# A Fourier layer and two expert layers on one core: tile sizes, conversion pace and the first blocks' order are changed

## The chip, the cores and the metric

The kernel runs on one core of one Trainium2 chip. The metric is the device time of one execution in microseconds. The profile is of one execution; its times are counted from the first instruction. PE is TensorE's matmul row and PEld its weight loads, DVE is VectorE, ACT is ScalarE, POOL is GpSimd, SP is SyncE, which issues all DMAs here.

## The reference

Two batches of 3008 tokens with 256 features go through a Fourier layer, and the 6016 tokens then through two expert layers with 2048 hidden features. The weights of the expert layers come as float64.

```python
X = np.fft.rfft(x, axis=1)                       # x: (2, 3008, 256)
Yr = Xr @ w_r - Xi @ w_i + b_r
Yi = Xr @ w_i + Xi @ w_r + b_i
Yr, Yi = sign(Y) * max(abs(Y) - 0.01, 0)         # each of the two
y = np.fft.irfft(Yr + 1j * Yi, n=3008, axis=1)
h = y.reshape(6016, 256) @ w_in                  # first expert layer
y1 = (h * np.cos(h)) @ w_out
h = y1 @ w_in2                                   # second expert layer
out = (h * np.clip(h + 3, 0, 6) / 6) @ w_out2
```

## The kernel before

Every product is made of float32r halves: a tensor `a` is kept as `hi` (rounded) and `lo` (the rest), and a product is hi·hi + hi·lo + lo·hi, three matmuls of 128 rows, 128 columns of weights and up to 512 moving columns.

**Transform.** 3008 = 47·64. For each batch, stage A (`a_part`, L334) multiplies eight chunks of x with a table: 16 short matmuls a chunk with 96 moving columns; the result goes to `zh`, `zl`. Then twelve steps `k2_step` work on two frequencies each. A step has twelve matmuls `w_mm` (L398, moving operand `wh` or `wl`), six `b_mm` (L421, moving `ph`), three `v_mm` (L452, moving `sh` or `sl`). Between them ACT and DVE split, add the bias and shrink; `shrink_lo` (L446) forms `sl` on POOL. `v_store` sends a block to DRAM (`u_dram`). What is left of the last steps (`drain`, a list of twelve pieces) is done one piece after each `a_part` of the next batch, or between the first units of the expert layers. `load_u` fetches a group of the transform's output and its table (`u_sb`, `tg_sb`), `y_part` (L286) makes 376 tokens of it, half of the features at a time, into the token tiles `y_sb`. Block 0 of 512 tokens needs groups 0 and 1, block 1 group 2 as well.

**Conversion.** Each expert weight is turned from float64 bits into hi and lo by `convert`. A chunk is 128x512 values; either layer has 16. A step of `Converter` issues one of five DVE instructions (clamp L154, shift L157, top L160, exponent L163, rest L166); with them go ACT's magnitude (L151) and hi (L170) and POOL's sum (L167) and lo (L173). After `rest` the next chunk is loaded into a `raw` tile, 512 KB. `RATE_A`, `RATE_W` say how many steps go with each `a_part` and each k2 step below `PW`; `RATE_1`, `RATE_2` how many go with each unit of the expert layers, `RATE_1` for the units of the first layer on blocks 0 to 2. `cv.require` does at once what a matmul needs and is not yet converted. Before: 34 steps in each batch's twelve k2 steps and 9 in stage A, 77 in all, or 15 chunks.

**Expert layers.** A unit is one block of tokens (eleven of 512, one of 384) and one of 16 groups of 128 hidden features: six matmuls `mm_h` (L577, moving operand the token tiles), the activation on ACT and DVE, a split into `gh` (ACT L620) and `gl` (DVE L621), and, four units later, six matmuls `mm_out` (L634, moving operand `gh`, `gl`, `gh` twice). `groups` orders the units: blocks 0, 1, 2 of the first layer alone, then a block of the first and one of the second layer in turns, unit by unit, and the second layer's last three alone.

PE, ACT and SP take their instructions in the order in which the code issues them; DVE's and POOL's are put in order by the framework's planner.

**Place in SBUF.** The tiles of the pool `persist` stand one behind another; a size is rounded up to 32 bytes per partition. Up to `first` every tile starts at 128 bytes past a multiple of 512. `first` has 8 bytes, which take 32. So `raw`, `cva`, `cvb`, `gh`, `gl`, `o`, `u_sb` and `tg_sb`, which follow it, start at remainder 160; `sh` and `sl` share the slots of `gh` and `gl`. `tg_sb` has 1504 bytes, and 1504 + 32 is a multiple of 512: what follows it (`zh`, `ph`, `wh`, the later token tiles, the second layer's weights) is at 128 again, as are the first layer's weights and the first token tiles.

Of the kernel before, what the change touches and what calls it, by code (L numbers as in the profile page):

```python
# [9 lines left out]
F32 = mybir.dt.float32  # L10
F32R = mybir.dt.float32r
BF16 = mybir.dt.bfloat16
I32 = mybir.dt.int32
U32 = mybir.dt.uint32
AF = mybir.ActivationFunctionType
ALU = mybir.AluOpType
# [9 lines left out]
TP = 2 * N1  # L26
ROWS = 2 * DOF
LAM = 0.01
TWO_PI = 2.0 * math.pi
YPAIRS = 4  # L30
BLOCK_TOKENS = [512] * 11 + [384]
A_CHUNKS = [4] * 8
NFC = DFF // 128
LEAD = 3
DELAY = 4
WARM = 9


RATE_A = (0, 1)
RATE_W = (1, 2, 2)  # L40
RATE_1 = ((1, 0),) * 7 + ((0, 0),)
RATE_2 = ((1, 0), (1, 1))
LATE, CC, CV0 = [1, 3, 4], 5, 7
XB = 3
PW = 12
YP = (0, 3, 6)
YE = 3


# [64 lines left out]
def fourier_moe_moe_kernel(ctx, tc, x, w_r, w_i, b_r, b_i, ta, tg, fg, win1, wout1, win2, wout2, out):  # L114
    nc = tc.nc
    pe, act, dve, sp = nc.tensor, nc.scalar, nc.vector, nc.sync

    def f32(ap):
        return ap.bitcast(F32)

    persist = ctx.enter_context(tc.tile_pool(name="persist", bufs=1))
# [13 lines left out]

    def convert(src, dst_hi, dst_lo, name):

        raw = persist.tile([128, 512, 2], I32, tag="raw", bufs=3, name=f"raw{name}")
        a = persist.tile([128, 512], F32, tag="cva", bufs=2, name=f"cva{name}")
        b = persist.tile([128, 512], F32, tag="cvb", bufs=1, name=f"cvb{name}")  # L140
        au, bu = a.bitcast(U32), b.bitcast(U32)
        w_lo, w_hi = raw.bitcast(U32)[:, :, 0], raw.bitcast(U32)[:, :, 1]

        def load():
            if len(src.shape) == 2:
                sp.dma_start(raw.rearrange("p f two -> p (f two)"), src)
            else:
                sp.dma_start(raw.rearrange("p (a f) two -> p a (f two)", a=2), src)

        def magnitude():  # L150
            act.activation(a, raw.bitcast(F32)[:, :, 1], AF.Abs)  # L151

        def clamp():
            dve.tensor_scalar(a, a, T_MIN, T_MAX, op0=ALU.max, op1=ALU.min)  # L154

        def shift():
            dve.tensor_scalar(au, au, 3, 0x3FFFFFF8, op0=ALU.logical_shift_left, op1=ALU.bitwise_and)  # L157

        def top():
            dve.scalar_tensor_tensor(au, w_hi, 0xC0000000, au, op0=ALU.bitwise_and, op1=ALU.bitwise_or)  # L160

        def exponent():
            dve.tensor_scalar(bu, au, 0xFF800000, None, op0=ALU.bitwise_and)  # L163

        def rest():
            dve.scalar_tensor_tensor(b, w_lo, float(2.0**-52), b, op0=ALU.mult, op1=ALU.mult)  # L166
            nc.gpsimd.tensor_tensor(a, a, b, op=ALU.add)  # L167

        def hi():
            act.activation(dst_hi, a, AF.Copy)  # L170

        def lo():
            nc.gpsimd.tensor_tensor(dst_lo, a, f32(dst_hi), op=ALU.subtract)  # L173

        return dict(load=load, magnitude=magnitude, clamp=clamp, shift=shift, top=top, exponent=exponent, rest=rest, hi=hi, lo=lo)
# [78 lines left out]
    YT = YPAIRS * TP  # L254
# [5 lines left out]
    def groups_of(j):  # L260

        return range(-(-starts[j] // YT), -(-starts[j + 1] // YT))

    u_sb, tg_sb, y_sb, x1_sb = {}, {}, {}, {}


    def token_set(pool, i):
        return [[pool.tile([128, MAXT], F32R, name=f"tok{i}_{e}{z}") for z in range(2)] for e in range(2)]

    free_sets = [token_set(persist, i) for i in range(2)]  # L270

    def load_u(g):
        if g >= NG:
            return
        b, p0 = divmod(g * YPAIRS, NPAIR)
        ut = persist.tile([ROWS, YPAIRS, D], F32, tag="u_sb", name=f"u_sb{g}")
        sp.dma_start(ut, u_dram[b][:, :, p0 : p0 + YPAIRS, :].rearrange("s f i e -> (s f) i e"))
        tt = persist.tile([ROWS, YT], F32, tag="tg_sb", name=f"tg_sb{g}")
        sp.dma_start(tt, tg[:, p0 * TP : (p0 + YPAIRS) * TP])
        u_sb[g], tg_sb[g] = ut, tt  # L280

    def y_part(g, ec):

        yp = psum.tile([128, 512], F32, tag="h", bufs=4, name=f"yp{g}_{ec}")
        for i in range(YPAIRS):
            pe.matmul(  # L286
                yp[:, i * TP : (i + 1) * TP],
                lhsT=u_sb[g][:, i, ec * 128 : (ec + 1) * 128],
                rhs=tg_sb[g][:, i * TP : (i + 1) * TP],
                start=True,  # L290
                stop=True,
            )
        for j in range(NBLK):
            t0, t1 = max(g * YT, starts[j]), min((g + 1) * YT, starts[j + 1])
            if t0 < t1:
                if j not in y_sb:
                    y_sb[j] = free_sets.pop(0)
                yh, yl = (z[:, t0 - starts[j] : t1 - starts[j]] for z in y_sb[j][ec])
                src = yp[:, t0 - g * YT : t1 - g * YT]
                act.activation(yh, src, AF.Copy)  # L300
                dve.tensor_tensor(yl, src, f32(yh), op=ALU.subtract)
        if ec == 1:
            load_u(g + 1)


    with ExitStack() as actx:
        apool = actx.enter_context(tc.tile_pool(name="apool", bufs=1))
        with tc.manual_schedule(engines={mybir.EngineType.PE, mybir.EngineType.SP, mybir.EngineType.Activation}):
# [4 lines left out]
            for b in range(NB):  # L313
                p0 = 0
# [35 lines left out]
            warm = persist.tile([128, 2, D], BF16, tag="r", bufs=3, name="warm")  # L350
            dve.memset(warm, 0.0)

            first = persist.tile([128, 2], F32, name="first")
            act.activation(first, warm[:, 0, 0:2], AF.Sin)
            wp = psum.tile([128, 2, D], F32, tag="acc0", bufs=2, name="wp")
            for i in range(WARM):
                pe.matmul(wp, lhsT=warm[:, 0, 0:128], rhs=warm, start=True, stop=True)
# [28 lines left out]
            ph_t, pp_t, bp_t, u_t, sh_t, vp_t = {}, {}, {}, {}, {}, {}  # L386
# [42 lines left out]
            def shrink_a(b, p):  # L429

                u_t[b, p] = persist.tile([128, 2, D], F32, tag="r", bufs=3, name=f"u{b}_{p}")
                act.activation(u_t[b, p], bp_t[b, p], AF.Relu, bias=-LAM, scale=1.0)  # L432
# [10 lines left out]

            def shrink_lo(b, p):
                sh, sl = sh_t[b, p]
                nc.gpsimd.tensor_tensor(sl, u_t.pop((b, p)), f32(sh), op=ALU.subtract)  # L446

            def v_mm(b, p):
                vp = psum.tile([128, 2, D], F32, tag="acc1", bufs=2, name=f"vp{b}_{p}")
# [16 lines left out]
            def k2_step(b, p):  # L466
                if p < NP:
                    w_mm(b, 2 * p)
                if p >= 2:
                    bias_add(b, p - 2)  # L470
                    shrink_a(b, p - 2)
                    cv.step(RATE_W[0] if p < PW else 0)
                    shrink_b(b, p - 2)
# [9 lines left out]
                if p < NP:  # L483
                    w_mm(b, 2 * p + 1)
                    cv.step(RATE_W[1 + p % 2] if p < PW else 0)
                    w_split(b, 2 * p + 1)
# [21 lines left out]
            for b in range(NB):  # L508
# [16 lines left out]
                for p in range(NP):  # L525
                    if b == NB - 1 and p == YP[0]:
                        load_u(0)
                    k2_step(b, p)
                    if b == NB - 1 and p in YP[1:]:
                        y_part(*divmod(YP[1:].index(p), 2))  # L530
                    if b == 0 and 6 <= p < 6 + XB:
                        load_x(NA + p - 6)
                pend = drain(b)
            pend.pop(0)()
            y_part(1, 0)
            pend.pop(0)()
            y_part(1, 1)
            pend.pop(0)()
            pend.pop(0)()


    mpool = ctx.enter_context(tc.tile_pool(name="mpool", bufs=1))
    with tc.manual_schedule(engines={mybir.EngineType.PE, mybir.EngineType.SP, mybir.EngineType.Activation}):
        free_sets += [token_set(mpool, i) for i in range(2, LEAD + 3)]

        groups = [[(0, j)] for j in range(LEAD)]
        groups += [[(0, j), (1, j - LEAD)] for j in range(LEAD, NBLK)] + [[(1, j)] for j in range(NBLK - LEAD, NBLK)]
        order, units, events = [], [], {}
        for i, group in enumerate(groups):
            g0, n0 = len(units), len(order)  # L550
            order += group
            for q in range(NFC):
                units += [(n0 + n, *job, q) for n, job in enumerate(group)]
            size = len(units) - g0
            if i + 1 < len(groups) and groups[i + 1][0][0] == 0:
                parts = [(g, e) for g in groups_of(groups[i + 1][0][1]) for e in range(2)]
                for k, (g, e) in enumerate(reversed(parts)):
                    events.setdefault(g0 + size - YE - 2 * k, []).append(lambda g=g, e=e: y_part(g, e))
# [65 lines left out]
        def mm_out(g):  # L624
# [7 lines left out]
            for d in range(2):  # L632
                for i, (w, r) in enumerate(((oh, gh), (oh, gl), (ol, gh))):
# [4 lines left out]
                        start=(fc == 0 and i == 0),  # L638
                        stop=(fc == NFC - 1 and i == 2),
                    )  # L640
# [19 lines left out]
        for g in range(G + DELAY):  # L660
            if g < G:
                n, m, j, fc = units[g]
                cv.require(("in", m, fc // 4, 0))
                cv.require(("in", m, fc // 4, 1))
                mm_h(g)
                if fc == NFC - 1:
                    free_sets.append((y_sb if m == 0 else x1_sb).pop(j))
# [6 lines left out]
            if g < G:  # L674
                rate = RATE_1[g % 8] if units[g][2] < LEAD and units[g][1] == 0 else RATE_2[units[g][1]]
            cv.step(rate[0])
# [6 lines left out]
            if 0 <= g - DELAY < G:  # L683
                n2, m2, _, fc2 = units[g - DELAY]
                cv.require(("out", m2, fc2 // 2))
                mm_out(g - DELAY)
                if fc2 == NFC - 1:
                    finish(n2, 0)
# [46 lines left out]
```

## Time and profile before

| | before |
|---|---|
| median of 3 runs | 1277.17 us (1274.96 to 1279.31) |
| the profiled execution | 1280.78 us, span 1279.0 us |
| PE busy | 1258.8 us, 98% |
| PEld busy | 1039.5 us, 81% |
| DVE busy | 823.9 us, 64% |
| ACT busy | 789.0 us, 62% |
| POOL busy | 116.3 us, 9% |
| mean granted clock | 0.988 |

The profiled execution took 1.8 us more than its span, and 3.6 us more than the median of the runs. Busy shares are means over stages that differ; a busy PE says only that matmuls follow one another, not how closely.

### The profile page before, as it was taken

Reading aid. Unit: us, or ns where it says so; the run is one execution under the profiler, and the core shown is the slowest. Engines: PE = TensorE matmul, PEld = TensorE weight load, DVE = VectorE, ACT = ScalarE, POOL = GpSimd, SP = SyncE. Lnnn points to the kernel's source line nnn. Section 1 sums busy time; section 2 is a strip of 40 time slices with the busy share of each in tenths; the row PEclk is TensorE's granted clock in tenths of the full one; section 3 lists DMA queues with packets and bytes.
Section 4 is the critical chain, followed back from the end, with each engine's and each line's share of the span. In section 5 each row is a group of like instructions: output and inputs, shape, how many; then the busy total and the mean of one; then the engine's idle time right before and its main releaser. Section 6 shows DMA issues by size and latency. Waiting matters only on the chain.

```text
span 1279.0 us, 15606 instructions
## 1 busy us (share of the span) xinstructions
PE 1258.8 (98%) x5633; PEld 1039.5 (81%) x5633; DVE 823.9 (64%) x1331; ACT 789.0 (62%) x1474; POOL 116.3 (9%) x92
## 2 busy tenths in 40 slices
PE   9988999999999999999999999999999999999998
PEld 8867877888888888888888888888888888888888
DVE  4887798888887655655555655655656556554444
ACT  4555567888777656656666666665656656654443
POOL 0342452111132000000000000000000000000000
PEclk9996999999999999999999999999999999999999
DMA  7255353111110100100100001000000000000000
GB/s 217 59 142 151 90 142 83 51 44 57 51 56 12 34 1 18 34 1 1 34 1 18 17 1 34 17 1 18 17 1 18 17 1 17 1 1 17 17 1 29
DMA packets 25117, 48.53 MB, mean 38 GB/s; under 512 B 2768, under 2 KB 12880, under 8 KB 25040
## 3 DMA queue, kind: packets, MB, share of 16 engines
q1 hardware_dynamic: 25040, 47.54, 13.1%
q8 instruction: 44, 0.72, 0.2%
q14 instruction: 33, 0.27, 0.1%
HBM read 35.08 MB, written 12.45 MB: 37 GB/s over the span
## 4 chain that ended last, share of the span: by engine, by line
PE 90%; DVE 6%; ACT 2%; issue 1%; DMA 1%; POOL 0%; SPq 0%; POOLq 0%; ACTq 0%; DVEq 0%
PE acc L634 41%; PE h L577 40%; PE zp L334 3%; PE pp L398 2%; PE yp L286 2%; DMA x<-in_x_dram 1%; DVE ph L412 1%; PE bp L421 1%; DVE bp L427 1%; DVE u L436 1%; DVE cvb0i L166 1%; PE vp L452 1%; DVE cvb0o L166 0%; ACT u L432 0%; DVE cva0o L154 0%
## 5 line engine op out<-in xcount | busy, mean ns | idle before, releaser
L612 DVE SCALAR_TENSOR_TENSOR h<-r,h 128x512 f32<-128x512 f32 (+1 forms) x192 | 131.4, 685 | 261.8 <-ACT r L593 261.7
L577 PE MATMUL h<-tok,w1i 128*128 128x512 f32 (+1 forms) x1152 | 294.2, 391 | 1.8 <-DVE gl L621 1.7
L577 PE MATMUL h<-tok,w2i 128*128 128x512 f32 (+1 forms) x1152 | 291.6, 388 | 0.0
L634 PE MATMUL acc<-gh,w1o 128*128 128x512 f32 (+1 forms) x768 | 270.2, 392 | 0.0
L634 PE MATMUL acc<-gh,w2o 128*128 128x512 f32 (+1 forms) x768 | 269.5, 392 | 0.0
L621 DVE TENSOR_TENSOR gl<-h,gh 128x512 fp32r<-128x512 f32 (+1 forms) x384 | 258.3, 673 | 0.8 <-ACT gh L620 0.8
L577 PEld LDWEIGHTS h<-tok,w1i 128*128 128x128 f32 x1152 | 213.3, 188 | 47.9 <-DVE gl L621 2.5
L577 PEld LDWEIGHTS h<-tok,w2i 128*128 128x128 f32 x1152 | 215.2, 188 | 45.5
L593 ACT ACTIVATE r<-h 128x512 f32<-128x512 f32 (+1 forms) x192 | 113.0, 589 | 185.7 <-PE h L577 185.6
L620 ACT ACTIVATE gh<-h 128x512 fp32r<-128x512 f32 (+1 forms) x384 | 224.7, 585 | 0.8 <-PE acc L634 0.5
L589 DVE SCALAR_TENSOR_TENSOR r<-r,h 128x512 f32<-128x512 int32 (+1 forms) x192 | 129.9, 677 | 123.0 <-ACT r L588 122.3
L588 ACT ACTIVATE r<-h 128x512 int32<-128x512 f32 (+1 forms) x192 | 113.4, 590 | 148.8 <-PE h L577 146.5
L634 PEld LDWEIGHTS acc<-gh,w2o 128*128 128x128 f32 x768 | 144.3, 188 | 31.4
L634 PEld LDWEIGHTS acc<-gh,w1o 128*128 128x128 f32 x768 | 144.3, 188 | 31.4
L634 PE MATMUL acc<-gl,w2o 128*128 128x512 f32 (+1 forms) x384 | 149.2, 389 | 0.0
L634 PE MATMUL acc<-gl,w1o 128*128 128x512 f32 (+1 forms) x384 | 149.2, 388 | 0.0
L601 ACT ACTIVATE r<-r 128x512 f32<-128x512 f32 (+1 forms) x192 | 120.0, 625 | 37.6 <-DVE r L589 37.5
L610 DVE TENSOR_TENSOR h<-r,h 128x512 f32<-128x512 f32 (+1 forms) x192 | 129.5, 674 | 0.0
L609 ACT ACTIVATE r<-r 128x512 f32<-128x512 f32 (+1 forms) x192 | 120.2, 626 | 0.0
L634 PEld LDWEIGHTS acc<-gl,w1o 128*128 128x128 f32 x384 | 72.0, 187 | 15.3
L634 PEld LDWEIGHTS acc<-gl,w2o 128*128 128x128 f32 x384 | 72.0, 188 | 15.0
L334 PEld LDWEIGHTS zp<-ta,x 96*128 96x128 f32 x256 | 50.0, 302 | 5.8 <-issue 4.5
(79 smaller groups left out, 959.8 us busy)
## 6 DMA issues: line engine op xcount, KB each, us to landing
x<-in_x_dram SPq DMA_DIRECT2D x16, 384.0 KB, 5.2
u_dram<-v SPq DMA_DIRECT2D x48, 128.0 KB, 2.4
u_sb<-u_dram SPq DMA_DIRECT2D x16, 384.0 KB, 3.8
out_dram<-o SPq DMA_DIRECT2D x22, 256.0 KB, 2.2
raw0i<-in_win_dram SPq DMA_DIRECT2D x8, 512.0 KB, 4.6
raw0o<-in_wout_dram SPq DMA_DIRECT2D x8, 512.0 KB, 4.3
raw1i<-in_win_dram SPq DMA_DIRECT2D x8, 512.0 KB, 3.6
raw1o<-in_wout_dram SPq DMA_DIRECT2D x8, 512.0 KB, 3.9
```

What stands on the lines that cost most here:

```text
L334: pe.matmul(zp[:, i * ROWS : (i + 1) * ROWS], lhsT=x_t[a][:, i, kc * 128 : (kc + 1) * 128], rhs=ta_t[a][:, i * ROWS : (i + 1) * ROWS], sta ...
L577: pe.matmul(hp[:, :t], lhsT=w[:, c0 : c0 + 128], rhs=r[:, :t], start=(i == 0), stop=(i == 5))
L588: act.activation(k[:, :t], hp[:, :t], AF.Copy, bias=0.0, scale=1.0 / TWO_PI)
L589: dve.scalar_tensor_tensor(r[:, :t], k[:, :t], -TWO_PI, hp[:, :t], op0=ALU.mult, op1=ALU.add)
L593: act.activation(r[:, :t], hp[:, :t], AF.Relu, bias=3.0, scale=1.0)
L601: act.activation(mid[g][:, :t], mid[g][:, :t], AF.Abs)
L609: act.activation(r[:, :t], r[:, :t], AF.Sin, bias=math.pi / 2, scale=-1.0)
L610: dve.tensor_tensor(hp[:, :t], r[:, :t], hp[:, :t], op=ALU.mult)
L612: dve.scalar_tensor_tensor(hp[:, :t], r[:, :t], 6.0, hp[:, :t], op0=ALU.min, op1=ALU.mult)
L620: act.activation(gh[:, :t], hp[:, :t], AF.Copy)
L621: dve.tensor_tensor(gl[:, :t], hp[:, :t], f32(gh[:, :t]), op=ALU.subtract)
L634: pe.matmul(acc[n][d][:, :t], lhsT=w[:, fc % 2, d * 128 : (d + 1) * 128], rhs=r[:, :t], start=(fc == 0 and i == 0), stop=(fc == NFC - 1 an ...
```

## The change

`first` and `tg_sb` are made multiples of 512 bytes, so that every tile starts at remainder 128. `raw` has two slots for three, a third set of token tiles is in `persist` and one less in `mpool`. Conversion steps: 23 in the first ten k2 steps of a batch, none in the last two, so 55 with stage A's 9; 11 with every eight units of blocks 0 to 2 for 7. `sl` is formed on DVE. Group 1's two `y_part` go into k2 steps 6 and 8 of the second batch (group 0's into 2 and 4), group 2's into the drain. Blocks 0 and 1 of the first layer take turns, four units each.

```diff
+TILE = 128
-RATE_W = (1, 2, 2)
-RATE_1 = ((1, 0),) * 7 + ((0, 0),)
+RATE_W = (1, 1, 2)
+RATE_1 = ((1, 0), (1, 0), (1, 0), (1, 1), (1, 0), (1, 1), (1, 0), (1, 1))
-PW = 12
-YP = (0, 3, 6)
+PW = 10
+YP = (0, 2, 4, 6, 8)
@@ convert
-        raw = persist.tile([128, 512, 2], I32, tag="raw", bufs=3, name=f"raw{name}")
+        raw = persist.tile([128, 512, 2], I32, tag="raw", bufs=2, name=f"raw{name}")
@@
-    free_sets = [token_set(persist, i) for i in range(2)]
+    free_sets = [token_set(persist, i) for i in range(3)]
@@ load_u
-        tt = persist.tile([ROWS, YT], F32, tag="tg_sb", name=f"tg_sb{g}")
-        sp.dma_start(tt, tg[:, p0 * TP : (p0 + YPAIRS) * TP])
+        tt = persist.tile([ROWS, -(-YT // TILE) * TILE], F32, tag="tg_sb", name=f"tg_sb{g}")
+        sp.dma_start(tt[:, 0:YT], tg[:, p0 * TP : (p0 + YPAIRS) * TP])
@@
-            first = persist.tile([128, 2], F32, name="first")
-            act.activation(first, warm[:, 0, 0:2], AF.Sin)
+            first = persist.tile([128, TILE], F32, name="first")
+            act.activation(first[:, 0:2], warm[:, 0, 0:2], AF.Sin)
@@ shrink_lo
-                nc.gpsimd.tensor_tensor(sl, u_t.pop((b, p)), f32(sh), op=ALU.subtract)
+                dve.tensor_tensor(sl, u_t.pop((b, p)), f32(sh), op=ALU.subtract)
@@ after the second batch's k2 steps
-            y_part(1, 0)
+            y_part(2, 0)
             pend.pop(0)()
-            y_part(1, 1)
+            y_part(2, 1)
@@
-        free_sets += [token_set(mpool, i) for i in range(2, LEAD + 3)]
-        groups = [[(0, j)] for j in range(LEAD)]
+        free_sets += [token_set(mpool, i) for i in range(3, LEAD + 3)]
+        groups = [[(0, 0), (0, 1)]] + [[(0, j)] for j in range(2, LEAD)]
@@
-            for q in range(NFC):
-                units += [(n0 + n, *job, q) for n, job in enumerate(group)]
+            step = 4 if i == 0 else 1
+            for q in range(NFC // step):
+                units += [(n0 + n, *job, q * step + f) for n, job in enumerate(group) for f in range(step)]
```

## Rows read from the trace of the kernel before

**Rows 1.** Windows by stage: stretch, its us, each engine's busy us (instructions), clock, DMA

```profile
33.30:95.00 61.70, 58.16 (x240) 45.20 (x240) 52.50 (x79) 34.34 (x64) 26.96 (x20) 1.00 0.40 104
95.00:129.30 34.30, 28.62 (x145) 26.21 (x143) 24.07 (x32) 19.30 (x29) 10.06 (x8) 0.66 0.57 149
129.30:190.70 61.40, 58.84 (x256) 47.05 (x256) 52.55 (x78) 36.69 (x69) 30.14 (x22) 0.97 0.43 116
190.70:208.24 17.54, 14.73 (x63) 11.31 (x61) 12.35 (x23) 11.68 (x26) 6.39 (x5) 0.90 0.37 91
208.24:1275.60 1067.36, 1066.86 (x4803) 881.14 (x4801) 666.34 (x1104) 671.91 (x1271) 42.56 (x33) 1.00 0.06 20
```

**Rows 2.** Timeline of PE, two units of 512 columns: start us, us, instructions

```profile
425.45 1.55 PE L577 MATMUL h<-tok,w2i 128*128 128x512 f32 x6
426.83 0.40 PE L634 MATMUL acc<-gh,w2o 128*128 128x512 f32 x1
...
428.23 1.55 PE L577 MATMUL h<-tok,w1i 128*128 128x512 f32 x6
...
431.02 1.55 PE L577 MATMUL h<-tok,w2i 128*128 128x512 f32 x6
```

**Rows 3.** Timeline of PE in a k2 step without a wait

```profile
54.66 1.52 PE L421 MATMUL bp<-ph,fgr 128*128 128x512 f32 x6
56.02 0.39 PE L398 MATMUL pp<-wh,zh 128*128 128x512 f32 x1
...
57.38 0.40 PE L452 MATMUL vp<-sh,fgr 128*128 128x512 f32 x1
...
58.09 0.39 PE L398 MATMUL pp<-wh,zh 128*128 128x512 f32 x1
```

**Rows 4.** Timeline of PE, one unit of the last block, 384 columns

```profile
1258.71 1.21 PE L577 MATMUL h<-tok,w2i 128*128 128x384 f32 x6
1259.76 0.33 PE L634 MATMUL acc<-gh,w2o 128*128 128x384 f32 x1
...
1260.79 1.21 PE L577 MATMUL h<-tok,w2i 128*128 128x384 f32 x6
```

**Rows 5.** Waits: who waited for whom, us in total, times, longest

```profile
PEld vp L452 <- POOL sl L446: 9.0, 9, 2.6
```

**Rows 6.** Lines by form: count, busy us, mean ns, idle before

```profile
L446 POOL TENSOR_TENSOR sl<-u,sh 128x512 fp32r<-128x512 f32 x24 | 31.9, 1327 | 48.1 <-ACT sh L441 48.1
L427 DVE TENSOR_TENSOR bp<-bp,bias 128x512 f32<-128x512 f32 x24 | 16.5, 689 | 0.1
L166 DVE SCALAR_TENSOR_TENSOR cvb0i<-raw0i,cvb0i 128x512 f32<-128x512 uint32 x8 | 9.5, 1189 | 0.2
L160 DVE SCALAR_TENSOR_TENSOR cva0i<-raw0i,cva0i 128x512 uint32<-128x512 uint32 x8 | 5.5, 684 | 0.1
L157 DVE TENSOR_SCALAR cva0i<-cva0i 128x512 uint32<-128x512 uint32 x8 | 5.4, 678 | 0.2
L163 DVE TENSOR_SCALAR cvb0i<-cva0i 128x512 uint32<-128x512 uint32 x8 | 5.3, 656 | 0.1
L154 DVE TENSOR_SCALAR cva0i<-cva0i 128x512 f32<-128x512 f32 x8 | 5.1, 637 | 3.2 <-ACT cva0i L151 3.2
```

**Rows 7.** Windows around the second batch's stage A, as in rows 1

```profile
105.60:112.40 6.80, 5.56 (x44) 4.91 (x43) 5.76 (x7) 4.96 (x9) 2.56 (x2) 1.00 0.50 128
112.40:132.90 20.50, 18.66 (x75) 17.23 (x76) 12.30 (x16) 10.98 (x18) 5.06 (x4) 0.50 0.74 196
```

**Rows 8.** Timeline of the same stage: start us, us, instruction [idle before it]

```profile
97.53 0.67 ACT L151 ACTIVATE cva0o<-raw0o 128x512 f32<-128x512 f32 x1 [0.92 <-POOL w1i L173]
...
98.74 0.76 PE L421 MATMUL bp<-ph,fgr 128*128 128x512 f32 x1 [1.83 <-ACT ph L411]
...
109.43 0.42 SPq L327 DMA_DIRECT2D x<-in_x_dram  x1
...
114.24 5.41 PE L334 MATMUL zp<-ta,x 96*128 96x96 f32 x24 [2.78 <-DMA x<-in_x_dram]
```

**Rows 9.** Window of the first units of the expert layers, as in rows 1

```profile
208.00:222.00 14.00, 14.00 (x62) 11.34 (x61) 13.45 (x22) 13.21 (x26) 2.60 (x2) 1.00 0.30 83
```

## The prediction

> **What bounds the kernel now.** I read the windows by stage first [rows 1]. The expert layers, from 208.24 us on, take 1067.4 of the span, and PE is busy in all but 0.5 of it, at the full clock of 2.4 GHz; DVE and ACT are busy for 62 and 63%. There only PE's own pace can change the time. The transform takes the first 208 us, and PE does not fill it: four stages between 33.3 and 208.24 us have something to give.
>
> Next I read PE's pace from start to start in the timeline, since a busy PE does not tell it. Two units take 431.02 - 425.45 = 5.57 us, 2.785 each: 1.38 for the six `mm_h`, 1.40 for the six `mm_out` [rows 2]. In a k2 step six matmuls of the same 512 columns take 56.02 - 54.66 = 1.36 (`b_mm`) and 57.38 - 56.02 = 1.36 us (half of `w_mm`), but the three `v_mm` 0.71 [rows 3]. So one matmul takes 0.227 us with moving operand `ph`, `wh` or `wl`, and 0.233 to 0.237 with `sh`, `sl`, `gh`, `gl`. The first kind starts at remainder 128, the second at 160; clock, columns and weights' remainder are the same. `mm_h` has its moving operand at 128 and yet takes 0.230: every six of them follow six of the other kind. I read this as a pace that a matmul at 160 upsets and that settles only after some matmuls at 128. One thing speaks against it: with 384 columns the two kinds take 1.05 and 1.03 us, with no loss at 160 [rows 4].
>
> Last I read the transform's waits: `v_mm` waits for POOL's `sl`, 9.0 us in nine waits [rows 5], and stage A of the second batch runs much of its time at the half clock, 1.2 GHz [rows 7].
>
> **The change part by part.** *Remainders.* All twelve matmuls of a unit then have their operands at 128. At the k2 pace a unit takes 12 x 0.2267 = 2.72 us, 0.065 less; there are 11 x 16 x 2 = 352 units of 512 columns, so 22.9 us. I take **-22**, as the units behind a `y_part` start unsettled. Bounds: 0, if the remainder is not the cause, and +5, if all twelve came to run like `mm_out` (2.80 x 352 against 2.785 x 352). I choose the upper end because `b_mm` and `w_mm` follow one another at 0.227 with DVE and ACT at work beside them.
>
> The page "SBUF — State Buffer" of the Trainium skill (Specifications) gives SBUF lines of 16 bytes, and "TensorE: Matmul & The Clock Gate" (Back-to-back issue gap) a gap of N / 2.4 + 2.5 ns, 216 for N = 512, that knows no address. 128 and 160 are both multiples of 16, so by these pages this part would be worth nothing, and the sum 22 us higher; the trace shows neither 216 nor one gap for all.
>
> *k2 steps.* A conversion step costs DVE (0.637 + 0.678 + 0.684 + 0.656 + 1.189) / 5 = 0.77 us [rows 6]. Now a k2 step has four other DVE operations at 0.69 and 34 / 12 conversion steps: 2.76 + 2.18 = 4.94 us, beside PE's 21 x 0.227 = 4.76. Then it is 5 x 0.69 + 2.3 x 0.77 = 5.22 in ten steps and 3.45 in the last two: 59.1 us a loop for 59.2. DVE's sum stays, but its last two steps are free, and POOL loses 24 x 1.33 = 31.9 us [rows 6]. The price of `sl` on DVE is not in the trace; the nearest are two other operations with both inputs in SBUF, `top` at 0.684 and `rest` at 1.189 [rows 6]. I take 0.69, like `top`, since POOL has a third less to do; at the other end 24 x 0.5 = 12 us more lie on DVE.
>
> The same page of the skill (Who interferes with whom) says that a DVE instruction with two SBUF inputs and a GpSimd instruction that reads SBUF lock each other out. `rest` at 1.189 beside `top` at 0.684 agrees in part; by it `sl` would tend to the dear end.
>
> The first loop takes 61.7 us for 240 matmuls worth 240 x 0.2267 = 54.4, so 7.3 are lost; the second, with 16 short ones at about 0.126 (5.56 / 44, rows 7), loses 61.4 - 54.4 - 2.0 = 5.0 [rows 1, 7]. Its wait for POOL goes; next late is DVE, which is about as long as PE. I take **-3** and **-1** (the second loop gets two `y_part` more than before on a full DVE); bounds -5 to +3 each, the loss being the 0.46 us by which 5.22 exceeds 4.76, in some seven steps.
>
> *Stage A of the second batch.* ACT is held by POOL's lo of a conversion at 97.53, so `ph` comes late, PE idles 1.83 us before `b_mm`, and the low clock follows [rows 8]. With no conversion in steps 10 and 11 that wait should go, worth its 1.83 and half of the slow 6.8 us that follow until 105.60: **-5**. Then PE waits 2.78 us for x, whose DMA is issued at 109.43 behind a `v_store` on SP's queue [rows 8], and 20.5 us pass at the half clock, 249 ns a matmul against 126 [rows 7]. That order on SP is not changed, so I expect that wait again. If it vanished, up to 10 more would be gained; if the first stays, 0.
>
> *Drain into the experts.* 63 matmuls in 17.54 us at clock 0.90 [rows 1]; 47 at 0.227 and 16 at 0.126 make 12.7, so about 5 are lost. DVE comes to it with less left over: **-2.5** (0 to -4).
>
> *First expert units.* 48 units get 66 steps for 42, half a step more each: at most 0.5 x 0.77 = 0.38 us on DVE. The fullest stretch has DVE busy 13.45 of 14 us, 2.68 a unit [rows 9]; 3.06 would exceed 2.72 by 0.34. All 48 so would cost 16 us; but that stretch also holds the transform's last pieces, so I charge five units, **+1.5**.
>
> *At nothing:* two raw slots: a load then waits on SP for `rest` and must land a chunk, five steps or two k2 steps (9.5 us), later; the x load above took 4.8 [rows 8]. What stands behind it on SP is `v_store`, `load_x`, `load_u`; without the cover each late chunk holds ACT's magnitude for the difference. Ten chunks instead of 15: with blocks 0 and 1 in turns the 11th is first needed at unit 20, after 27 more steps where it needs 4; the 14th at unit 24, with 33 for 19. Without turns unit 8 would need the 9th and unit 12 the 13th. The moved `y_part` are the same matmuls on PE, taken from the expert stage and added to the transform.
>
> Sum: -22 - 3 - 1 - 5 - 2.5 + 1.5 = -32, from 1280.8 to 1248.8. The profiled execution lies above all three runs, by 3.6 us over their median; I take off half of it: **1247 us**.
>
> **The rivals.** *The remainder is not the cause* (0.13): `sh`, `sl`, `gh`, `gl` share tags as well as remainder, and the 384 columns show no loss [rows 4]. Then -10 remain: 1269. This is also where the skill's 16-byte lines lead.
>
> *The pace is gained, the transform gives nothing* (0.19): DVE at 5.22 a step keeps both loops where they are, and the clock falls at the same places. -22 + 1.5 and nothing else: 1260 before the offset, 1258 after it.
>
> *`sl` blocks DVE* (0.05), the other side: in the transform each `sl` waits for a POOL instruction as long as its own, 1.33 us, on top of 0.69, and all 24 lie on the path, as DVE has no room in ten of twelve steps: 24 x 1.33 = +32, which also takes the transform's gains; with -22 + 1.5 that is 1292, 1290 after the offset. It decides against the change from about 0.9 us per `sl` on the path (21 / 24). For it: `rest` at 1.189. Against it: POOL works 27 of 61.7 us in the loop [rows 1], of which `sl` itself was 16, so a random `sl` meets it a fifth of the time.
>
> **How the numbers follow.** My forecast has 0.63, its own range 1238 to 1256: downward most of the ten us of stage A's second wait, upward the loops and the early units. 1234 to 1265 adds 4 us of the loops' lower bounds below, takes in the second rival and leaves out the first, the third and a tail. A measurement of this kernel can tell about 0.3%, 4 us. Faster: forecast, second rival and half of the first, 0.89; the rest of the first, with a loss in the loops, 0.06 for the same; slower 0.05.
>
> **What would show it.** Right: six `mm_out` and six `mm_h` in 1.36 us each and 2.72 a unit; no wait for `sl` on POOL; `v_mm` at 0.68 for three; the full clock through the last `b_mm` of the first batch; the expert stage near 1046 us long, PE without idle in its first 48 units. Wrong: `mm_out` still at 1.40; `sl` above 0.9 us; `b_mm` waiting for DVE in the k2 steps; waits of `mm_h` on the activation in the first 48 units; SP holding a raw load in front of x. The step that I trust least is `sl`: the planner decides where DVE's queue has it, and a `v_mm` behind a late `sl` holds the next `w_mm` on PE, as [rows 5] show of POOL.

## The result, and the profile after

The changed kernel takes 1241.63 us (median of 4 runs, 1238.83 to 1242.94) for 1276.07 before (4 runs, 1274.78 to 1279.31): a ratio of 0.9723, 95% interval 0.9697 to 0.975. The profiled execution took 1241.19 us, its span is 1239.4.

The windows by stage of the changed kernel, with the same borders in the work as in [rows 1] (first `w_mm`, second batch's stage A, its first `w_mm`, the `y_part` behind the last k2 step, first `mm_out`, end):

```profile
30.64:86.72 56.08, 56.08 (x239) 45.81 (x239) 48.20 (x81) 34.84 (x63) 11.88 (x9) 0.96 0.37 105
86.72:114.80 28.08, 25.11 (x144) 24.00 (x143) 22.41 (x32) 17.19 (x25) 2.61 (x3) 0.74 0.67 176
114.80:173.57 58.77, 58.77 (x272) 48.56 (x272) 50.34 (x86) 36.86 (x70) 14.12 (x11) 0.98 0.41 106
173.57:187.64 14.07, 12.39 (x62) 10.16 (x61) 10.02 (x19) 10.66 (x23) 1.26 (x1) 1.00 0.39 95
187.64:1235.95 1048.31, 1046.56 (x4787) 878.75 (x4785) 679.35 (x1122) 676.92 (x1275) 53.70 (x42) 1.00 0.07 22
```

Against [rows 1]: the expert stage is 19.1 us shorter, the k2 loops 5.6 and 2.6, stage A of the second batch 6.2, the drain 3.5. In both loops PE is now busy in every microsecond. That makes 37.0; another 2.4 us lie in the first batch's stage A, in which the change alters no instruction: it took 23.7 to 27.8 us in the fourteen profiled executions of this study. What differs there is the pace. From 5 to 14 us PE did 41 of the stage's short matmuls in the kernel before and 64 in the changed one. The five executions with 39 to 43 of them there took 27.3 to 27.8 us for the stage (before, no_pad, sl_pool, old_pace, no_turns), the nine with 64 or 65 took 23.7 to 25.4. No edit sorts them: sl_pool and no_turns issue the same instructions in that stage as the changed kernel. So these 2.4 us are put down to chance. The profiled execution of before took 4.7 us more than the median of its runs, that of the changed kernel 0.4 less, so the medians differ by 34.4 only.

PE's timeline in two units of 512 columns, beside [rows 2]:

```profile
431.14 1.52 PE L580 MATMUL h<-tok,w1i 128*128 128x512 f32 x6
432.50 0.39 PE L637 MATMUL acc<-gh,w1o 128*128 128x512 f32 x1
...
433.86 1.52 PE L580 MATMUL h<-tok,w2i 128*128 128x512 f32 x6
...
436.58 1.52 PE L580 MATMUL h<-tok,w1i 128*128 128x512 f32 x6
```

Six `mm_h` in 1.36 us, six `mm_out` in 1.36, a unit in 2.72 for 2.785. And the three `v_mm` of a k2 step, beside [rows 3], now 0.68 for 0.71:

```profile
59.52 0.39 PE L453 MATMUL vp<-sh,fgr 128*128 128x512 f32 x1
...
60.20 0.39 PE L399 MATMUL pp<-wh,zh 128*128 128x512 f32 x1
```

### The profile page after: what moved, and what is told of

The parts are those of the page before. It is cut to its first block, busy times and chain, and to the rows that moved or that the text cites. A ratio compares the mean times of both kernels' runs of the same rounds, so it can differ in the third digit from the quotient of the medians.

```text
span 1239.4 us, 15550 instructions
## 1 busy us (share of the span) xinstructions
PE 1224.5 (99%) x5633; PEld 1029.7 (83%) x5633; DVE 826.7 (67%) x1355; ACT 792.4 (64%) x1474; POOL 83.8 (7%) x68
## 4 chain that ended last, share of the span: by engine, by line
PE 93%; DVE 2%; DMA 2%; ACT 1%; issue 1%; SPq 0%; ACTq 0%; DVEq 0%
PE h L580 40%; PE acc L637 39%; PE pp L399 6%; PE bp L422 3%; PE zp L335 2%; PE yp L287 2%; DMA x<-in_x_dram 2%; PE vp L453 1%; DVE h L613 1%; DVE gl L624 0%; DVE r L592 0%; DVE cvb1i L164 0%; ACT r L612 0%; ACT v L458 0%; ACT r L591 0%
## 5 line engine op out<-in xcount | busy, mean ns | idle before, releaser
L580 PE MATMUL h<-tok,w2i 128*128 128x512 f32 (+1 forms) x1152 | 287.7, 385 | 0.0
L637 PE MATMUL acc<-gh,w1o 128*128 128x512 f32 (+1 forms) x768 | 264.2, 385 | 0.0
L637 PE MATMUL acc<-gh,w2o 128*128 128x512 f32 (+1 forms) x768 | 263.6, 385 | 0.0
L637 PEld LDWEIGHTS acc<-gh,w1o 128*128 128x128 f32 x768 | 144.0, 188 | 27.7
L335 PE MATMUL zp<-ta,x 96*128 96x96 f32 x256 | 43.9, 349 | 6.8 <-DMA x<-in_x_dram 6.1
```

Source lines behind the costliest of these rows:

```text
L580: pe.matmul(hp[:, :t], lhsT=w[:, c0 : c0 + 128], rhs=r[:, :t], start=(i == 0), stop=(i == 5))
L637: pe.matmul(acc[n][d][:, :t], lhsT=w[:, fc % 2, d * 128 : (d + 1) * 128], rhs=r[:, :t], start=(fc == 0 and i == 0), stop=(fc == NFC - 1 an ...
```

## The experiments

The theory: a moving operand at remainder 160 upsets PE's pace, worth about 20 us; the rest comes from the transform, from `sl` off POOL and from fewer conversion steps. The rivals: the pace has another cause; DVE becomes the bound of the k2 steps; SP's order undoes the gain. Stage times below, in us, are from PE's first instruction of a stage to that of the next, in the profiled execution of each kernel. The second loop ends here with its last `w_mm`; the `b_mm` of its last step, 1.4 us, count to the drain, other than in [rows 1].

| kernel | stage A, first | k2, first | stage A, second | k2, second | drain | experts |
|---|---|---|---|---|---|---|
| before | 27.8 | 61.7 | 34.3 | 60.0 | 19.0 | 1067.2 |
| changed | 25.4 | 56.1 | 28.1 | 57.4 | 15.5 | 1048.2 |
| no_pad | 27.3 | 56.7 | 27.7 | 57.8 | 15.5 | 1067.2 |
| pad_only | 24.1 | 60.8 | 33.7 | 59.8 | 19.0 | 1048.0 |
| sl_pool | 27.3 | 59.1 | 27.4 | 59.0 | 16.6 | 1047.9 |
| sl_dve_only | 24.5 | 56.2 | 29.4 | 56.3 | 16.3 | 1067.2 |
| old_pace | 27.3 | 55.6 | 29.3 | 57.5 | 15.6 | 1055.8 |
| no_turns | 27.3 | 55.5 | 27.6 | 57.4 | 15.5 | 1060.9 |
| late_store | 24.3 | 55.7 | 24.7 | 59.4 | 15.5 | 1048.1 |

**The padding undone, and the padding alone.**

```diff
# no_pad, from the changed kernel; pad_only is the reverse, from the kernel before
# (the two lines that use these tiles change with them and are left out)
-            first = persist.tile([128, TILE], F32, name="first")
+            first = persist.tile([128, 2], F32, name="first")
-        tt = persist.tile([ROWS, -(-YT // TILE) * TILE], F32, tag="tg_sb", name=f"tg_sb{g}")
+        tt = persist.tile([ROWS, YT], F32, tag="tg_sb", name=f"tg_sb{g}")
```

> The changed kernel with first and tg_sb at their old sizes, so that gh, gl, sh, sl and the other tiles behind first stand at remainder 160 again. If the remainder sets PE's pace: a unit takes 2.785 us again, the expert stage is 20 to 23 us longer, and the kernel about 1241.6 + 22 = 1264 us. If the pace comes from anything else in the change (order of units, sl on DVE, slots): still 2.72 a unit and about 1242 us.

> The kernel before with the two padded tiles alone. If the remainder sets PE's pace: 2.72 us a unit and 1276 - 22 = 1254 us, and the transform as before, with its waits for sl on POOL. If it works only together with the rest of the change: 2.785 and about 1276 us.

Measured: no_pad 1261.58 us, 0.9875 of before (0.9849 to 0.9901); pad_only 1256.82 us, 0.9845 (0.9826 to 0.9864). The expert stages by windows, first no_pad, then pad_only:

```profile
190.40:1257.70 1067.30, 1066.53 (x4787) 878.24 (x4785) 680.44 (x1122) 676.80 (x1275) 53.89 (x42) 1.00 0.07 22
```

```profile
202.30:1250.20 1047.90, 1047.15 (x4803) 880.95 (x4801) 665.65 (x1104) 672.26 (x1270) 42.40 (x33) 1.00 0.06 20
```

Both came out within 3 us of what was expected if the remainder sets the pace (1264 and 1254). PE is busy throughout in both and the numbers of instructions hardly differ; the two padded tiles alone move the stage by 19.0 us (no_pad beside the changed kernel) and 19.2 (pad_only beside the kernel before), whatever else is in the kernel. With the tiles padded, the changed kernel's other edits together move the stage by 0.2 us (1048.0 in pad_only, 1048.2 in the changed kernel).

**Which remainder.** Three kernels move the tiles behind `first` further from the rest, and two move the weights.

```diff
# rem64: 16 elements for 64 bytes; rem128: 32; rem256: 64
-            first = persist.tile([128, TILE], F32, name="first")
+            first = persist.tile([128, 16], F32, name="first")
# tg_sb gets 112 elements more; 96 in rem128, 64 in rem256
-        tt = persist.tile([ROWS, -(-YT // TILE) * TILE], F32, ...
+        tt = persist.tile([ROWS, -(-YT // TILE) * TILE + 112], F32, ...
# all_160: ahead of every other tile; w1_160: the same, and first,
# with TILE - 8 elements, right behind the first layer's weights
+    lead = persist.tile([128, 8], F32, name="lead")
+    dve.memset(lead, 0.0)
```

> The changed kernel with the tiles behind first 64 bytes further on, at remainder 192 by 512, all others at 128. If one remainder by 512 is what counts: 2.785 us a unit, about 1264 us. If a start at a multiple of 64 is enough: 2.72 a unit, about 1242.

> The same with 256 bytes, remainder 384. One remainder by 512: 2.785 us a unit, about 1264. A multiple of 64 or 128 is enough: 2.72, about 1242.

> The changed kernel with the tiles behind first 128 bytes further on, at remainder 256. 32 bytes cost 65 ns a unit, 64 bytes 53 ns, 256 none. If the distance counts by 128 bytes: 2.72 us a unit, expert stage 1048 us. If it counts by 256: above 2.72, expert stage 1055 to 1067 us.

> The changed kernel with a tile of 32 bytes ahead of all others, so that every tile, weights and moving operands, stands at remainder 160. If equal remainders of weights and moving operand are what counts: 2.72 us a unit, about 1242 us. If the moving operand's own start counts: all twelve matmuls of a unit are of the slow kind, 2.785 or more, 1264 us or more.

> The changed kernel with the first layer's weights alone at remainder 160, the second layer's and all moving operands at 128. If the weights' remainder against the moving operand's counts: units of the first layer at 2.785 us, of the second at 2.72, about 1253 us. If only the moving operand's start counts: both 2.72, about 1242.

In the three rem kernels the longer `tg_sb` brings what follows it back to 128. Each of these five kernels was measured in one execution, so the unit's pace and the stage decide, not the total (the last column; for changed and no_pad it is the median of four). The remainders by 512 follow from the sizes of the tiles; the slices that a matmul reads of a weight tile lie at multiples of 512 bytes in it.

| kernel | remainder of weights, of moving operands of `mm_h`, of `mm_out` | us, six `mm_h` + six `mm_out` | expert stage us | whole kernel us |
|---|---|---|---|---|
| changed | 128, 128, 128 | 1.36 + 1.36 | 1048.2 | 1241.6 |
| no_pad | 128, 128, 160 | 1.38 + 1.40 | 1067.2 | 1261.6 |
| rem64 | 128, 128, 192 | 1.39 + 1.38 | 1063.1 | 1252.8 |
| rem128 | 128, 128, 256 | 1.38 + 1.39 | 1061.7 | 1254.8 |
| rem256 | 128, 128, 384 | 1.36 + 1.36 | 1048.2 | 1240.9 |
| all_160 | 160, 160, 160 | 1.36 + 1.36 | 1048.5 | 1240.1 |
| w1_160, first layer | 160, 128, 128 | 1.39 + 1.40 | 1060.5 | 1252.0 |
| w1_160, second layer | 128, 128, 128 | 1.37 + 1.37 | | |

The timeline of all_160, then of w1_160, PE:

```profile
432.41 1.52 PE L583 MATMUL h<-tok,w2i 128*128 128x512 f32 x6
433.77 0.39 PE L640 MATMUL acc<-gh,w2o 128*128 128x512 f32 x1
...
435.13 1.52 PE L583 MATMUL h<-tok,w1i 128*128 128x512 f32 x6
```

```profile
430.60 1.53 PE L583 MATMUL h<-tok,w2i 128*128 128x512 f32 x6
431.97 0.39 PE L640 MATMUL acc<-gh,w2o 128*128 128x512 f32 x1
...
433.34 1.56 PE L583 MATMUL h<-tok,w1i 128*128 128x512 f32 x6
434.73 0.40 PE L640 MATMUL acc<-gh,w1o 128*128 128x512 f32 x1
...
436.13 1.07 PE L583 MATMUL h<-tok,w2i 128*128 128x512 f32 x4
```

All at 160 is as good as all at 128. With every moving operand at 128 and the first layer's weights at 160, that layer is slow and the other, in turns with it, nearly at the full pace. So it is not the moving operand's own start: what counts is the distance between the starts of the weights and of the moving operand. Of the distances tried, 32 (either way), 64 and 128 bytes cost; 256 costs nothing. The remainder by 256 would have been enough. 64 bytes met neither of the two figures expected (1264 and 1242): they cost, but less than 32. The other four kernels each met one of the two outcomes expected. The timeline of rem128:

```profile
433.92 1.54 PE L580 MATMUL h<-tok,w1i 128*128 128x512 f32 x6
435.30 0.40 PE L637 MATMUL acc<-gh,w1o 128*128 128x512 f32 x1
...
436.69 1.54 PE L580 MATMUL h<-tok,w2i 128*128 128x512 f32 x6
```

There `mm_h` has no distance and yet takes 1.38: it starts unsettled behind `mm_out`, as in [rows 2]. Matmul by matmul, in the mean of the 176 units of the second layer of rem128, the six `mm_h` take 231, 232, 230, 227, 227 and 227 ns, each from its start to the next start; in the changed kernel all six take 227.

**`sl` back on POOL, and `sl` on DVE alone.**

```diff
# sl_pool, from the changed kernel; sl_dve_only is the reverse, from the kernel before
-                dve.tensor_tensor(sl, u_t.pop((b, p)), f32(sh), op=ALU.subtract)
+                nc.gpsimd.tensor_tensor(sl, u_t.pop((b, p)), f32(sh), op=ALU.subtract)
```

> The changed kernel with sl on POOL again. If the wait for sl on POOL was what the k2 steps lost: waits of v_mm come back, the two loops are 3 to 8 us longer together, about 1246 to 1250 us. If fewer conversion steps alone freed the loops: within 1 us of 1242.

> The kernel before with sl on DVE alone. If POOL's sl is what the k2 steps of before wait for: the first loop at 56 us for 61.7, the second near 58, 10 to 16 us gained in the transform, about 1262 to 1266 us. If DVE, with 5 x 0.69 + 34/12 x 0.77 = 5.63 us a step, becomes the bound: the loops at 62 us or more, 1277 to 1290 us.

Measured: sl_pool 1247.46 us, 0.9767 of before (0.9745 to 0.9789), within what was expected; sl_dve_only 1260.12 us, 0.9867 (0.9844 to 0.9891), 2 us better than expected. The waits of sl_pool show the old wait again; PE's own part of it was 5.6 us in five waits in the kernel before:

```profile
PEld vp L453 <- POOL sl L447: 5.3, 8, 1.2
PE vp L453 <- POOL sl L447: 2.2, 5, 0.8
```

In sl_dve_only the first loop has no idle time on PE, although DVE got `sl` on top of all 34 conversion steps; the window of that loop, and `sl` and `rest` among its lines by form:

```profile
29.70:85.90 56.20, 56.20 (x240) 45.23 (x240) 51.08 (x87) 35.55 (x66) 16.11 (x12) 0.97 0.45 114
```

```profile
L446 DVE TENSOR_TENSOR sl<-u,sh 128x512 fp32r<-128x512 f32 x24 | 18.3, 764 | 0.6
...
L166 DVE SCALAR_TENSOR_TENSOR cvb0i<-raw0i,cvb0i 128x512 f32<-128x512 uint32 x8 | 5.5, 687 | 0.1
```

This `rest` fell from 1.189 us [rows 6] to 0.687 once POOL had no `sl`. The 1.189 is a mean of two kinds. Of all 32 `rest` of before, the 21 that start while POOL is idle take 0.67 to 0.70 us; the 11 that start within a POOL instruction, `sl` five times and a conversion's `lo` six times, end 0.55 us behind the end of that one and take 1.35 to 1.78. One of each sort, from the trace of before; the `lo` starts as an `sl` of 71.92 to 73.53 ends:

```profile
54.91 1.34 POOL L446 TENSOR_TENSOR sl<-u,sh 128x512 fp32r<-128x512 f32 x1 [4.05 <-ACT sh L441]
55.13 1.67 DVE L166 SCALAR_TENSOR_TENSOR cvb0o<-raw0o,cvb0o 128x512 f32<-128x512 uint32 x1
...
73.48 1.48 POOL L173 TENSOR_TENSOR w1o<-cva0o,w1o 128x512 fp32r<-128x512 f32 x1
73.84 1.67 DVE L166 SCALAR_TENSOR_TENSOR cvb0i<-raw0i,cvb0i 128x512 f32<-128x512 uint32 x1
```

In sl_dve_only three of 32 start so, all behind a `lo` in the expert stage and none in the transform. "SBUF — State Buffer" of the Trainium skill (Who interferes with whom) says that a DVE instruction with two SBUF inputs contends with a GpSimd instruction that reads SBUF; the trace agrees for `rest` with both `sl` and `lo` on POOL. `rest` was dear because POOL was in an instruction when it started, and in the transform moving `sl` ended that: five of its eight dear `rest` stood behind `sl` itself, three behind a `lo`.

**The old pace, and no turns.**

```diff
# old_pace
-RATE_W = (1, 1, 2)
+RATE_W = (1, 2, 2)
-PW = 10
+PW = 12
-RATE_1 = ((1, 0), (1, 0), (1, 0), (1, 1), (1, 0), (1, 1), (1, 0), (1, 1))
+RATE_1 = ((1, 0),) * 7 + ((0, 0),)
# no_turns
-        groups = [[(0, 0), (0, 1)]] + [[(0, j)] for j in range(2, LEAD)]
+        groups = [[(0, j)] for j in range(LEAD)]
-            step = 4 if i == 0 else 1
+            step = 1
-            if i + 1 < len(groups) and groups[i + 1][0][0] == 0:
+            if 0 < i and i + 1 < len(groups) and groups[i + 1][0][0] == 0:
```

> The changed kernel with the conversion steps of before (34 for 23 in a batch's k2 steps, 7 for 11 with eight of the first units). If DVE's sum sets the k2 steps: 5 x 0.69 + 34/12 x 0.77 = 5.63 us a step for 4.76, up to 10 us a loop, and the idle before the last b_mm with the low clock behind it again: 1255 to 1265 us. If sl on DVE alone cured the waits: within 3 us of 1242.

> The changed kernel with blocks 0 and 1 one after the other, the y_part of block 2 within block 1's units. The 13th and 14th chunk are then needed at unit 12 instead of 24, three steps before the pace has them. If the turns are what keeps the fewer conversions hidden: PE waits in units 8 to 20, 2 to 8 us more, 1244 to 1250 us. If the pace is quick enough without them: 1240 to 1243 us.

Measured: old_pace 1249.86 us, 0.9791 of before (0.9774 to 0.9809); no_turns 1253.18 us, 0.981 (0.9792 to 0.9828).

In old_pace the k2 loops are as short as in the changed kernel, 55.6 and 57.5 us: with `sl` on DVE the number of conversion steps doesn't matter there, and the expectation from DVE's sum (10 us a loop) missed; nor did the kernel come within 3 us of 1242, the other figure expected. Its 8 us are lost in the expert stage, around one wait, behind which the granted clock stands at 0.50 until 269.9. PE's timeline, and SP's own waits around it:

```profile
264.16 1.99 PE L287 MATMUL yp<-tg_sb,u_sb 96*128 96x94 f32 x8 [7.81 <-DMA tg_sb<-in_tg_dram]
```

```profile
SPq L149 <- DVE cvb1i L167: 17.6, 1, 17.6
```

SP held a raw load for 17.6 us until DVE's `rest` had freed one of the two slots, and `load_u` stood behind it. That two slots cost something here where three would not is likely but not shown: no run has the old pace and the turns with three slots. In the changed kernel SP holds raw loads too, for 13.9 us at the longest, but PE never waits for `tg_sb` behind it.

In no_turns the expert stage takes 1060.9 us with PE idle for 7.8, in waits for the first layer's weights that come out of the conversion too late:

```profile
PE h L580 <- ACT w1i L171: 3.8, 1, 3.8
...
PE acc L637 <- ACT w1o L171: 2.2, 1, 2.2
```

Behind these waits the granted clock falls twice to 0.50:

```profile
214.20:221.00 6.80, 5.80 (x13) 4.11 (x14) 5.66 (x9) 3.32 (x6) 2.72 (x3) 0.50 0.45 151
238.10:244.90 6.80, 5.93 (x15) 4.45 (x14) 0.60 (x2) 0.94 (x2) 1.14 (x1) 0.50 0.19 70
```

The stage is 12.7 us longer than in the changed kernel. PE's idle time accounts for about 6 of them (7.8 us for 1.8), the half clock for about 5: its 28 matmuls keep PE busy for 11.7 us and would take 28 x 0.227 = 6.4 at the full clock. The expectation (2 to 8 us more) left the clock out. So the turns are what hides the five chunks that the new pace leaves to the expert stage.

**The stores behind the x loads.**

```diff
# late_store, in drain(b)
-                    lambda: (shrink_hi(b, p - 2), v_store(b, p - 3)),
+                    lambda: (shrink_hi(b, p - 2), b > 0 and v_store(b, p - 3)),
-                    lambda: shrink_b(b, p - 1),
+                    lambda: (shrink_b(b, p - 1), b == 0 and v_store(b, p - 3)),
-                    lambda: v_store(b, p - 2),
-                    lambda: None,
+                    lambda: b > 0 and v_store(b, p - 2),
+                    lambda: b == 0 and v_store(b, p - 2),
```

Two `v_store` of the first batch's drain go out later, each behind the x load that followed it.

> The changed kernel in which the first batch's drain issues each v_store after the x load of the next chunk on SP, not before it. In the changed kernel the x load waits on SP behind a v_store from 92.4 to 95.4 us, and PE then 2.82 us for x, with 17 us at the half clock behind it. If SP's order sets that wait: it shrinks to about 0.4 us; 2 us gained, and up to 8 more if the clock stays up, 1232 to 1240 us. If the DMAs' own landing sets it: 1241 to 1243 us.

In the changed kernel SP and PE stand so in that stage, by the timeline, and the window at the half clock follows:

```profile
93.44 1.23 SPq L460 DMA_DIRECT2D u_dram<-v  x2
94.77 0.54 SPq L326 DMA_DIRECT2D ta<-in_ta_dram  x1
95.36 0.42 SPq L328 DMA_DIRECT2D x<-in_x_dram  x1
...
99.98 1.25 PE L335 MATMUL zp<-ta,x 96*128 96x96 f32 x5 [2.82 <-DMA x<-in_x_dram]
```

```profile
100.10:117.20 17.10, 17.10 (x73) 15.84 (x73) 11.83 (x16) 7.89 (x10) 3.27 (x3) 0.50 0.65 173
```

In late_store the same load goes out at 91.51, ahead of the store at 93.85:

```profile
91.12 0.33 SPq L326 DMA_DIRECT2D ta<-in_ta_dram  x1
91.51 0.43 SPq L328 DMA_DIRECT2D x<-in_x_dram  x1
93.85 1.24 SPq L460 DMA_DIRECT2D u_dram<-v  x2
```

The wait for x did not go: it moved to the next chunk, whose load went out behind that store. PE's timeline of late_store, and its window at the half clock:

```profile
100.03 1.10 PE L335 MATMUL zp<-ta,x 96*128 96x96 f32 x8 [2.18 <-DMA x<-in_x_dram]
```

```profile
101.80:115.40 13.60, 12.82 (x51) 11.42 (x50) 8.98 (x13) 6.41 (x10) 1.97 (x3) 0.50 0.61 178
```

Measured 1239.35 us, 0.9707 of before (0.9682 to 0.9733). The wait is 2.18 us for 2.82, where 0.4 was expected: the time fell within what was expected, the mechanism did not. The half clock lasts 13.6 us for 17.1, but that says nothing of the order: rem64, with the changed kernel's order, has 13.6 us of it too, and rem256 20.5. Stage A falls from 28.1 to 24.7 us (26.4 in rem64), and the second loop loses 2 us of that again. Its interval overlaps that of the changed kernel (0.9697 to 0.975): whether it is faster, these runs can't tell.

## Why the prediction was right

The time, 1241.6 us for a forecast of 1247, lies in the range and in the forecast's own range, and the case was the forecast's: the pace and the transform both gave.

*Remainders, -22 with +1.5 for the early units.* Measured -19.1 in the expert stage, nearly the net of -20.5. Apart, the remainders gave -19.2 (pad_only) and the early units cost 0.2 (the changed kernel beside pad_only), so both terms were put too high by 1 to 3 us. The pace is the 0.2267 us that was read off the k2 steps. What failed is the reading behind it: not the moving operand's own remainder, but its distance from the weights' counts, as all_160 and w1_160 show. The rows of before could not tell the two apart, since all weights stood at 128. The 16-byte lines of the Trainium skill ("SBUF — State Buffer", Specifications) would have made 32 bytes free; here a unit takes 2.77 to 2.79 us with a distance of 32, 64 or 128 bytes and 2.72 without, and the measurement decides.

*k2 steps, -3 and -1.* Measured -5.6 and -2.6: right in direction, about half the size. The term mis-sized is DVE's price. It was put at 5.22 us a step, above PE's 4.76, but PE does not idle in the loops at all. A conversion step had been priced with POOL's `sl` in its way: in the first loop its five instructions take 0.76 us in the mean in the kernel before, 0.59 in sl_dve_only and old_pace, 0.53 in the changed kernel. And the recorded times of DVE's instructions overlap: the 86 that start in old_pace's first loop add up to 56.1 us and cover 51. So old_pace would need 5 x 0.69 + 34/12 x 0.59 = 5.1 us a step by the sum, and its steps take 4.6. `sl` itself cost 0.72 in the changed kernel, close to the 0.69 assumed.

*Stage A of the second batch, -5.* Measured -6.2, with the waits that were forecast: none before the last `b_mm`, then the same wait for x behind a `v_store`, 2.82 us, and the half clock after it. The reason given for the first, no conversion in steps 10 and 11, is only one of two that suffice. sl_pool has that and `sl` on POOL, and no wait there (27.4 us). sl_dve_only and old_pace convert in those steps with `sl` on DVE: ACT's late `ph` is gone, PE waits 1.28 and 1.31 us for DVE's, no half clock follows that wait, and the stage takes 29.4 and 29.3. pad_only, with neither, waits 1.86 and 1.04 us there and takes 33.7. One reading was rough: the 249 and 126 ns mix short matmuls with some of 512 columns; short ones alone take 213 at the half clock (40 from 120.78 to 129.29), and nothing in the sum hangs on the difference by more than 0.5 us. In late_store, where the store was moved, the wait moved to the next chunk (2.18 us): SP's order sets which chunk is late. The clock fell behind that wait too; whether a stage without any such wait keeps it stays open.

*Drain, -2.5.* Measured -3.5, at the full clock throughout.

*At nothing.* The two raw slots cost nothing that shows at the new pace; at the old one PE waits 7.8 us behind a load that lacked a slot. The fewer chunks cost nothing with the turns and 11.6 us without.

The second rival is out, the transform gave 17.9 us; the first, that the remainder is not the cause, by no_pad and pad_only; the third by sl_dve_only. One thing the prediction had wrong by omission: the gains were credited to several edits together, but the padding alone gives 20.0 us and `sl` on DVE alone 18.1 (1278.22 to 1260.12), more than the 34.4 of the whole; part of that excess is the first batch's stage A, which was short in the profiled executions of both (24.1 and 24.5 us). The pace, the turns, the slots and the moved `y_part` together add little once `sl` is on DVE: the four stages of the transform behind the first take 158.2 us in sl_dve_only and 157.1 in the changed kernel. With `sl` on POOL they do help, as sl_pool beside pad_only shows (162.1 us for 173.3, of which 27.4 for 33.7 in the second stage A); which of them, no run separates. A kernel with the padding and `sl` on DVE and nothing else was not run.

## What to carry to other kernels

Read PE's pace from start to start, six matmuls at a time: two groups of the same shape at 1.36 and 1.40 us are a cause to be found, and it can lie in where the tiles stand. Give tiles that feed matmuls sizes in multiples of 256 bytes, so that the starts of weights and moving operands stay a multiple of 256 apart, which cost nothing here. And before an operation is priced as a load on an engine, see whether its price is the blocking by the very instruction that is to be moved.

## What was not expected of the hardware

A distance of 32, 64 or 128 bytes between the starts of weights and moving operand costs 50 to 70 ns in twelve matmuls of 512 columns (2.77 to 2.79 us for 2.72), 256 none; what in the chip makes it so, and why the 384-column blocks of [rows 4] show no loss at 32, stays open. After such matmuls the pace needs some without a distance to settle, three in rem128. A `rest` on DVE that starts within a POOL instruction ends 0.55 us behind it; one that starts with POOL idle takes 0.69 in all. The same stage A took 23.7 to 27.8 us in fourteen executions, by the pace that PE had in its first microseconds; what decides that stays open.
